# Two of five threshold subtractions per attention pair moved from VectorE to GpSimd, with a new order of all tasks

## The chip, the cores and the metric

The kernel runs on one core of a Trainium2 chip. The metric is the device time of one execution in microseconds; lower is better. The kernel before takes 1224.37 us (median of 3 runs, 1223.91 to 1226.27). TensorE is called PE, its weight loads PEld, VectorE DVE, ScalarE ACT, GpSimd POOL and SyncE SP, as in the profile.

## The reference

An attention block with a threshold is followed by a feed-forward block; everything is float32.

```python
# q, k, v: (8, 8, 576, 64); tau = 0.02
scores = (q @ k.transpose(0, 1, 3, 2)) / 8
thresh = scores.max(-1, keepdims=True) - tau
scores = np.where(scores >= thresh, scores, -1e9)
attn = exp(scores - scores.max(-1, keepdims=True))
o = (attn / (attn.sum(-1, keepdims=True) + 1e-9)) @ v
x = o.transpose(0, 2, 1, 3).reshape(4608, 512)
h = x @ w_in                                   # 512 x 2048
out = (h / (1 + exp(-1.702 * h))) @ w_out      # 2048 x 512
```

## The kernel before, in words

**Attention.** Heads are taken two at a time: 32 pairs, four to a batch. The scores of a pair are computed transposed, key positions on the partitions, and stand in five tiles: tiles 0 to 3 hold 128 partitions x 1152 elements, tile 4 holds 128 x 576. For each pair the steps are:

- `load_qk`, `load_v` (SP issues the DMAs), then `prep` (DVE, L556) or, for pairs 0 to 3, a turn on PE (L565, L568) and copies (L578, L580);
- `scores_run`: PE (L590) into the PSUM pool psA, three buffers of two banks; `keep`: ACT copies each piece into its tile (L607);
- `in_groups`: DVE reduces each tile over groups of 32 (L613), here with max, later with add for the denominators; `over_tiles` (L622), `cross_max` (ACT, L632), `over_halves` (L639);
- `spread_max`: DVE writes the threshold of every query to the tile `mb` (L651), 128 x 576, one buffer for all pairs but 1 and 3;
- `sub`: each score tile minus `mb`, in place (L687); `mask`: ACT, a steep Prelu (L694); `exps`: ACT, Exp (L698);
- `values`: PE multiplies by v (L709) into psA; `place_x`: DVE multiplies by the reciprocal denominators (L813) and writes x, transposed, into the tiles xT.

From pair 7 on, the values of one pair and the scores of the next are interleaved on PE, tile by tile. Below, this stretch of PE is called a joint: 36 instructions of each kind, two records each in the trace.

**Feed-forward.** 18 blocks of 256 rows of x follow the pairs that fill them. The first two are plain products (L875, L886), whose hidden values pass through ACT (L843) and DVE (L892); the others use seven products instead of eight, in both layers, with sums formed on DVE. The first layer is L954, L1127 or L1278, the second L1431 or L1387; ACT copies (L968, L1168, L1292) and DVE adds (L973, L1173, L1295) take the first layer out of PSUM, and `read` (L1453 on DVE, L1446 on ACT) takes the second layer out. In blocks 7 to 12, POOL issues the DMAs that stream a set of weights (`w_flow`, L1104).

**Weights.** At the start, each 128 x 512 piece of w_in and w_out is rounded by two ACT instructions (`cv_power` L520, `cv_power2` L524) and two on DVE (L538, L545).

**Order.** Nothing is ordered by hand. Each step is a task with an engine, a cost in us, a rank and its dependencies; the kernel runs a planner (`run_in_order`) that plays the tasks through, gives each engine, whenever it falls free, the ready task of the lowest rank whose buffers are free, and issues the instructions in the order in which the tasks start. Engines then work through their queues strictly in that order. The rank is the pair's number plus a bias by the name of the step, from the tables EARLY (pairs 0 to 3), SECOND (4 to 7), LATER (the rest), CV (weights), and L_RANK and W_RANK (loads). PE's feed-forward work has the lowest priority and fills what attention leaves. Fillers (`stay_warm`, L1497) stand where the planner sees PE without work in the beginning.

```python
    def sub(n, t):
        s = sT[n, t].rearrange("p u h s -> p u (h s)")
        engine = nc.gpsimd if t in BY_POOL.get(n, ()) else nc.vector
        engine.tensor_tensor(
            out=s, in0=s, in1=mbs[n].unsqueeze(1).to_broadcast(list(s.shape)),
            op=ALU.add if n in BY_DMA else ALU.subtract,
        )
```

`BY_POOL` is empty before. For pairs 1 and 3 to 6 tiles 3 and 4 are subtracted by DMAs that add in memory (`add_row`, L678).

The buffer `mb` also takes the reciprocal denominators (`sums_in`, L785) of pairs 6 to 15 and 28 to 31: the planner lets a task start only if the units it takes of a buffer are free, and another task gives them back.

Of the kernel before, what the change touches and what calls it, by code (L numbers as in the profile page):

```python
# [32 lines left out]
def kernel(  # L33
# [40 lines left out]
    NKT = NK // 2  # L74
# [34 lines left out]
        for x in range(2)  # L109
# [26 lines left out]
    EARLY = {  # L136
        "add_row": 15.24,
        "cross_max": 16.53,
        "exps": 169.66,
        "in_groups": 24.3,  # L140
        "keep": 18.51,
        "load_qk": 52.9,
        "load_v": 77.19,
        "mask": 220.69,
        "one_row": 73.01,
        "over_halves": -24.07,
        "over_tiles": 93.0,
        "place_x": 110.06,
        "row_in": 2.01,
        "row_out": -23.95,  # L150
        "scores_run": 0.25,
        "spread_max": -9.31,
        "spread_sums": 55.95,
        "sub": 109.63,
        "sums_by_pe": 219.69,
        "turn_in": 106.44,
        "turn_rows": -16.16,
        "turned": 157.69,
        "values": 15.27,
    }  # L160
    SECOND = {
        "add_row": 48.97,
        "cross_max": -30.15,
        "cross_sums": 46.61,
        "exps": 425.25,
        "in_groups": 788.95,
        "keep": 52.62,
        "load_qk": -8.72,
        "load_v": 50.95,
        "mask": 273.1,  # L170
        "over_halves": 13.47,
        "over_tiles": 10.11,
        "place_x": -14.67,
        "prep": 130.42,
        "row_in": -47.42,
        "row_out": 60.46,
        "scores_run": -14.82,
        "spread_max": -16.4,
        "sub": 29.57,
        "sums_in": 53.13,  # L180
        "sums_out": -17.8,
        "turn_rows": -30.52,
        "turn_sums": 63.82,
        "values": -7.11,
    }
    LATER = {
        "add2": -163.47,
        "add3": -23.7,
        "copy2": 51.25,
        "copy3": 34.37,  # L190
        "cross_max": 60.81,
        "cross_sums": 61.03,
        "exps": 93.29,
        "in_groups": 10.85,
        "keep": 85.17,
        "load_qk": -13.0,
        "load_v": -2.27,
        "mask": 11.12,
        "over_halves": -26.94,
        "over_tiles": -36.69,  # L200
        "place_x": -13.68,
        "prep": 24.88,
        "s_level1": -6.85,
        "s_level2": -6.85,
        "scores_run": 22.76,
        "silu2": 83.51,
        "spread_max": -74.31,
        "sub": -0.09,
        "sums_in": -524.28,
        "sums_out": -75.26,  # L210
        "turn_sums": 83.71,
        "values": -57.82,
    }
    CV = {
        "cv_end": 69.28,
        "cv_power": -47.14,
        "cv_power2": -20.47,
        "cv_whole": -4.05,
        "load_w": 14.98,
    }  # L220

    LAG = {"PE": 0.26, "DVE": 0.18, "ACT": 0.22, "POOL": 0.18, "SP": 0.1}
# [136 lines left out]
    JOINT = 6  # L359
    SINGLE = 7  # L360
    TURNED = (0, 1, 2, 3)
    BY_POOL = {}

# [68 lines left out]
    def own(n, *pools):  # L432
        return tuple(x + "_apart" for x in pools) if n in APART else pools
# [1105 lines left out]
    for i in range(len(pieces)):  # L1539
        y = 0 if i < NDC else 2 if i < n_in else 4  # L1540
        n = NDC if i < NDC else n_in - NDC if i < n_in else n_in
# [14 lines left out]
        m = task("ACT", 0.75, rank, cv_power, i, after=[a] + over)  # L1556
        m = task("ACT", 0.56, rank, cv_power2, i, after=[m])
        if i in ROUND_BY_ACT:
            a = task("ACT", 0.65, rank, cv_round, i, after=[a])
# [760 lines left out]
            next_blk += 1  # L2320

    crossed = {"max": [], "sums": []}
    L_RANK = (6.9, -26.88, 69.44, 31.9, 9.2, 38.16, 10.43, 63.15, 25.98, 364.83, 169.13, -0.14, 11.11, -6.6, 5.42, 34.59, 27.46, 64.99, 61.43, -2.14, 71.89, -4.67, 27.56, 35.73)

    def load_rank(n, which):
        return L_RANK[3 * n + which] if 3 * n < len(L_RANK) else 0.0
# [16 lines left out]
    for n in range(NP):  # L2343
# [3 lines left out]
        r = float(n)  # L2347
# [102 lines left out]
        if n in BY_DMA:  # L2450
            a = task("DVE", 0.22, r, turn_rows, n, after=[a])
            a = transfer(rq[2], 0.3 + 0.4 * by_sp, task(rq[0], 0.65 * rq[1], r, row_out, n, after=[a]), lag=1.3 + flow)
            spread[n] = task(rq[0], 1.1 * rq[1], r, row_in, n, after=[a], take=own(n, "mb"))
# [115 lines left out]
```

## Time and profile before

| | us | share of the span |
|---|---|---|
| time, median of 3 runs | 1224.37 (1223.91 to 1226.27) | |
| span of the profiled execution | 1224.7 | |
| PE busy | 1206.5 | 99% |
| PEld busy | 995.8 | 81% |
| DVE busy | 1077.1 | 88% |
| ACT busy | 797.6 | 65% |
| POOL busy | 69.3 | 6% |

The profiled execution has no time of its own beside its span; the span stands 0.3 us above the median of the timed runs. Matmuls are pipelined, so a busy PE need not be at its peak. Rows of groups read: line, engine, operation, output and input with their shapes, count, then busy time in us and mean ns of one, then the idle time of the engine just before them and what ended it. Each PE instruction leaves two MATMUL records (the transposes of L565 one). Rows of the timeline read: start, duration, engine, line, operation, operands, count, and in brackets the idle time before. An order of instructions, engine by engine, can be read from the built programs of both kernels; it holds no times.

### The profile page before, as it was taken

The page shows a single profiled execution, that of the slowest core. Times are in us where ns is not written, and L with a number is a line of the kernel's source. Part 1 is how long each engine was busy: PE and PEld are TensorE (multiplying, and loading weights), DVE is VectorE, ACT ScalarE, POOL GpSimd, SP SyncE. Part 2 cuts the span into 40 slices and gives each one's busy share as a digit, 9 for nine tenths or more (in the row PEclk, how much of TensorE's full clock was granted, in tenths as well). Part 3 has the DMA queues.
Part 4 walks back from the last instruction along what each step waited for, and adds up shares of the span by engine and source line. Part 5 has one row for each costly group of instructions (what it writes and reads, how often), then busy time and mean ns, then how long its engine had stood idle before and what let it go on. Part 6 is the DMA issues. An engine that isn't in the chain of part 4 may idle for free.

```text
span 1224.7 us, 26240 instructions
## 1 busy us (share of the span) xinstructions
PE 1206.5 (99%) x10672; PEld 995.8 (81%) x10672; DVE 1077.1 (88%) x1683; ACT 797.6 (65%) x1197; POOL 69.3 (6%) x114
## 2 busy tenths in 40 slices
PE   8999999999999999999999999999999999999998
PEld 5656777797978888888777777787787797999998
DVE  6989998878898998898699977998799989999797
ACT  6999977675765766684686468756875676340340
POOL 0111231100000000000100010001100000000000
PEclk9999999999999999999999999999999999999999
DMA  8957769492323241224423252225322351444443
GB/s 222 249 108 190 173 142 170 103 210 65 93 50 110 49 120 48 75 72 135 101 67 99 66 133 72 59 77 128 92 49 67 87 139 39 139 129 140 140 137 104
DMA packets 201193, 136.09 MB, mean 111 GB/s; under 512 B 146864, under 2 KB 163376, under 8 KB 200944
## 3 DMA queue, kind: packets, MB, share of 16 engines
q1 hardware_dynamic: 189712, 110.21, 34.0%
q0 software_dynamic: 10672, 23.90, 9.4%
q8 instruction: 84, 1.38, 0.5%
q10 hardware_dynamic: 688, 0.30, 0.1%
q14 instruction: 37, 0.30, 0.1%
HBM read 103.28 MB, written 23.75 MB: 104 GB/s over the span
## 4 chain that ended last, share of the span: by engine, by line
PE 88%; ACT 8%; DMA 2%; DVE 1%; issue 1%; SPq 0%; DVEq 0%; ACTq 0%
PE ops L1431 28%; PE pv L709 10%; PE ps L590 10%; PE hps L954 7%; PE hps L1127 7%; PE ps L954 5%; PE ps L1127 5%; PE hps L1278 4%; PE ops L1387 4%; PE ps L1278 3%; PE ps L1387 3%; ACT arena L698 2%; ACT arena L694 2%; PE hps L886 2%; ACT arena L607 2%; DMA arena<-in_moe_w_in_dram 1%
## 5 line engine op out<-in xcount | busy, mean ns | idle before, releaser
L613 DVE TRANSPOSE_TENSOR_REDUCE part<-arena 128x36 f32<-128x1152 f32 x300 | 363.8, 1239 | 52.6 <-ACT arena L607 40.2
L607 ACT COPY arena<-ps 128x576 f32<-128x576 f32 x288 | 171.2, 642 | 95.6 <-PE ps L590 95.5
L694 ACT ACTIVATE arena<-arena 128x1152 f32<-128x1152 f32 (+1 forms) x160 | 164.6, 1064 | 66.6 <-DVE arena L687 66.2
L1431 PE MATMUL ops<-w_out,arena 128*128 128x256 f32 x896 | 203.0, 381 | 0.1
L1431 PEld LDWEIGHTS ops<-w_out,arena 128*128 128x128 f32 x896 | 168.5, 190 | 28.5 <-issue 5.3
L687 DVE TENSOR_TENSOR arena<-arena 128x1152 f32<-128x1152 f32 (+1 forms) x150 | 180.9, 1241 | 0.7
L698 ACT ACTIVATE arena<-arena,shift 128x1152 f32<-128x1152 f32 (+1 forms) x160 | 179.7, 1156 | 1.4
L590 PE MATMUL ps<-arena 64*64 64x288 f32 x2304 | 172.1, 408 | 8.0 <-ACT arena L607 6.1
L709 PE MATMUL pv<-arena 64*64 64x288 f32 x2176 | 159.2, 405 | 0.0
L590 PEld LDWEIGHTS ps<-arena 64*64 64x64 f32 x2304 | 81.9, 132 | 71.5 <-ACT arena L607 29.7
L1431 PE MATMUL ops<-arena 128*128 128x256 f32 x576 | 129.1, 379 | 0.0
L709 PEld LDWEIGHTS pv<-arena 64*64 64x64 f32 x2176 | 80.3, 133 | 53.0 <-issue 9.0
L1431 PEld LDWEIGHTS ops<-arena 128*128 128x128 f32 x576 | 109.2, 190 | 15.8 <-issue 0.9
L1292 ACT COPY arena<-hps 128x512 f32<-128x512 f32 x44 | 25.7, 584 | 59.5 <-PE hps L1278 59.5
L632 ACT ACTIVATE other<-red,minus_gap 32x18 f32<-32x18 f32 x118 | 36.2, 307 | 35.1 <-DVE red L622 33.6
L1104 POOL DMA_DIRECT2D arena<-wrow x36 | 19.5, 540 | 619.0 <-DVE arena L1197 321.8
L886 PE MATMUL hps<-xT,w_in 128*128 128x256 f32 x232 | 51.2, 381 | 0.9 <-DVE arena L892 0.9
L886 PEld LDWEIGHTS hps<-xT,w_in 128*128 128x128 f32 x232 | 43.6, 190 | 8.6 <-DVE arena L892 1.5
L1453 DVE SCALAR_TENSOR_TENSOR osb<-ops,osb 128x256 f32<-128x256 f32 x98 | 39.2, 411 | 11.5 <-PE ops L1431 10.5
L954 PEld LDWEIGHTS hps<-xT,w_in 128*128 128x128 f32 x384 | 44.2, 192 | 1.5 <-issue 0.9
L954 PE MATMUL hps<-xT,w_in 128*128 128x128 f32 x384 | 45.3, 276 | 0.0
L1127 PE MATMUL hps<-xT,w_in 128*128 128x256 f32 x192 | 43.4, 379 | 0.0
(228 smaller groups left out, 1859.9 us busy)
## 6 DMA issues: line engine op xcount, KB each, us to landing
arena<-in_v_dram SPq DMA_DIRECT2D x128, 144.0 KB
arena<-exu SPq DMA_DIRECT2D x42, 256.0 KB
arena<-ext SPq DMA_DIRECT2D x39, 256.0 KB
arena<-wrow POOLq DMA_DIRECT2D x36, 256.0 KB, 3.3
arena<-in_k_dram SPq DMA_DIRECT2D x112, 72.0 KB
arena<-in_q_dram SPq DMA_DIRECT2D x112, 72.0 KB
out_dram<-osb SPq DMA_DIRECT2D x28, 256.0 KB
arena<-row_s SPq DMA_DIRECT2D x48, 144.0 KB
```

Source lines behind the costliest of these rows:

```text
L590: nc.tensor.matmul(ps[ts(c, KT), h, 0:SH], lhsT=mats[n, 1][ts(h, D), ts(j, KT)], rhs=mats[n, 0][ts(h, D), ts(c, SH)], start=True, stop=True,)
L607: nc.scalar.copy(out=sT[n, t][:, u], in_=pss.pop((n, j))[:, :, 0:SH])
L613: nc.vector.tensor_reduce(out=stats[n, op][:, t * 2 * QB : min(2 * t + 2, NK) * QB], in_=sT[n, t].rearrange("p u h (g d) -> p (u h g) d", ...
L687: engine.tensor_tensor(out=s, in0=s, in1=mbs[n].unsqueeze(1).to_broadcast(list(s.shape)), op=ALU.add if n in BY_DMA else ALU.subtract,)
L694: nc.scalar.activation(out=s, in_=s, func=AF.Prelu, alpha=STEEP)
L698: nc.scalar.activation(out=s, in_=s, func=AF.Exp, scale=SCALE, bias=shift)
L709: nc.tensor.matmul(o[c][ts(h, D), 0:SH], lhsT=left(j, h)[ts(c, KT)], rhs=sT[n, t][ts(c, KT), u, h, :], start=(j == 0), stop=(j == NK - 1),)
L886: nc.tensor.matmul(hidden[j][:, ts(i, BLK)], lhsT=w_in[:, c, ts(j, P)], rhs=xTs[i][:, c, :], start=(c == 0), stop=(c == NDC - 1), skip_gro ...
L954: nc.tensor.matmul(o[:, ts(j, HT)], lhsT=left[:, c, ts(4 * y + j, P)], rhs=right[:, c, :], start=(x in (P1, P2, P5) and j + c == 0), stop= ...
L1127: nc.tensor.matmul(o[:, ts(j, BLK)], lhsT=left[:, c, ts(j, P)], rhs=right[:, c, :], start=(x in (P1, P2, P5) and j + c == 0), stop=(j + c ...
L1278: nc.tensor.matmul(o[:, ts(j, HT)], lhsT=left[:, ts(j, P)], rhs=right, start=(m in (P1, P2, P5) and j == 0), stop=(j == 3), skip_group_che ...
L1431: nc.tensor.matmul(banks[blk][k][:, ts(o, HM)], lhsT=left[:, j, :], rhs=right[:, j, :], start=(j == 0), stop=(j == HF - 1),)
```

## The change

For pairs 8 to 31 the subtraction of tiles 3 and 4 is issued on GpSimd; tiles 0 to 2 stay on DVE. The two chains no longer wait for each other, and `mb` counts as two units: `spread_max` takes both, the last subtraction on either engine gives one back. The denominators of later pairs (`sums_in`) still take one unit of `mb`. The planner books a GpSimd subtraction with 2.6 us for a full tile and 1.4 us for the last one. All biases of the ranks have new values, so the order of all tasks on all engines is another one. Which instructions are issued, and on what data, is otherwise the same.

```diff
-    for x in ("raw0", "raw1", "qkT0", "qkT1", "mb"):
+    for x in ("raw0", "raw1", "qkT0", "qkT1"):
         limits[x + "_apart"] = 1
+    limits["mb"] = limits["mb_apart"] = 2
     EARLY = {
-        "add_row": 15.24,
...
+        "add_row": -378.340771,
...
-    BY_POOL = {}
+    BY_POOL = {n: (3, 4) for n in range(8, 32)}
...
-    SHARED = 0.2 if BY_POOL else 0.0
...
-    W_RANK = (51.17, 144.32, 134.71, 686.68, 50.64, 279.44)
+    W_RANK = (-29.011801, 237.669982, 129.549423, 790.056925, 152.018894, 491.392438)
...
-            m = task("DVE", 0.78, r, spread_max, n, after=[a], take=own(n, "mb"))
+            m = task("DVE", 0.78, r, spread_max, n, after=[a], take=own(n, "mb") * 2)
         spread.setdefault(n, m)
-        ws, subs, last_add = [], [(m, None)], spread[n]
+        ws, last_add = [], spread[n]
         mine = ADDED.get(n, ())
+        behind_sub = {False: [m], True: [m]}
+        apart = BY_POOL.get(n, ())
+        by_vector = max(t for t in range(NKT + 1) if t not in mine and t not in apart)
+        by_two = {t: (t == by_vector) * (1 if apart else 2) + (t in apart[-1:]) for t in range(NKT + 1)}
         for t in range(NKT + 1):
...
+                pool = t in BY_POOL.get(n, ())
                 a = task(
-                    "DVE", 0.67 if tail else 1.27, r, sub, n, t, after=[y for y, _ in subs],
-                    give=own(n, "mb") if t == max(set(range(NKT + 1)) - set(mine)) else (),
+                    "POOL" if pool else "DVE", (1.4 if tail else 2.6) if pool else 0.67 if tail else 1.27, r, sub, n, t,
+                    after=behind_sub[pool], give=own(n, "mb") * by_two[t],
                 )
-                subs.append((a, None))
+                behind_sub[pool] = [a]
```

`SHARED` is used nowhere. The tables SECOND, LATER, CV and L_RANK change in the same way as EARLY and W_RANK. All lines of the changed kernel below the tables stand one further on (L590 is L591 there).

More of the change, by code (lines that the diff above doesn't have):

```diff
@@ L129 @@
               "raw0": 1, "raw1": 1, "qkT0": 1, "qkT1": 1, "v_m0": 1, "v_m1": 1, "w64_0": 1, "w64_1": 1, "row": 1, "row_s": 1, "rc": 1}
-    for x in ("raw0", "raw1", "qkT0", "qkT1", "mb"):
+    for x in ("raw0", "raw1", "qkT0", "qkT1"):
         limits[x + "_apart"] = 1
+    limits["mb"] = limits["mb_apart"] = 2
     limits["s_m_apart"] = NKT
     EARLY = {
-        "add_row": 15.24,
[L138 to L159, printed above, removed]
+        "add_row": -378.340771,
+        "cross_max": -51.670843,
+        "exps": -80.990469,
+        "in_groups": 24.707122,
+        "keep": -1679.732271,
+        "load_qk": -47.984891,
+        "load_v": 33.367154,
+        "mask": 240.776887,
+        "one_row": -544.415211,
+        "over_halves": -422.16303,
+        "over_tiles": -1679.661295,
+        "place_x": -112.949767,
+        "row_in": -35.770691,
+        "row_out": 917.119523,
+        "scores_run": -229.318419,
+        "spread_max": 320.427835,
+        "spread_sums": -32.4166,
+        "sub": 92.995208,
+        "sums_by_pe": 328.173046,
+        "turn_in": -142.452702,
+        "turn_rows": -201.348475,
+        "turned": 189.940288,
+        "values": 425.811909,
@@ L160 @@
     }
     SECOND = {
[L162 to L184, printed above, removed]
+        "add_row": 396.291781,
+        "cross_max": 134.376111,
+        "cross_sums": 254.096747,
+        "exps": 627.348081,
+        "in_groups": 1045.488067,
+        "keep": -1628.325603,
+        "load_qk": -155.794522,
+        "load_v": 99.246196,
+        "mask": 508.237893,
+        "over_halves": -20.868516,
+        "over_tiles": -152.960781,
@@ L185 @@
+        "place_x": 955.1794,
+        "prep": 343.422582,
+        "row_in": 96.454434,
+        "row_out": 125.121366,
+        "scores_run": -126.121027,
+        "spread_max": -35.804964,
+        "sub": 211.446055,
+        "sums_in": 50.193475,
+        "sums_out": -11.007232,
+        "turn_rows": 388.794059,
+        "turn_sums": 445.432231,
+        "values": -55.985049,
     }
     LATER = {
[L187 to L209, printed above, removed]
@@ L210 @@
-        "sums_out": -75.26,
-        "turn_sums": 83.71,
-        "values": -57.82,
+        "add2": -1112.316868,
+        "add3": -1680.126556,
+        "copy2": 64.472372,
+        "copy3": -15.546448,
+        "cross_max": -210.684879,
+        "cross_sums": 950.298394,
+        "exps": 665.775135,
+        "in_groups": 26.792662,
+        "keep": -1855.554282,
+        "load_qk": -101.543529,
+        "load_v": -530.802781,
+        "mask": 92.181036,
+        "over_halves": -26.986143,
+        "over_tiles": -46.863265,
@@ L213 @@
+        "place_x": 35.133329,
+        "prep": 730.714298,
+        "s_level1": -38.984452,
+        "s_level2": -38.984452,
+        "scores_run": 22.464676,
+        "silu2": -1261.340063,
+        "spread_max": 9.276515,
+        "sub": -15.906025,
+        "sums_in": -660.343636,
+        "sums_out": 434.369551,
+        "turn_sums": 447.129924,
+        "values": 217.876057,
     }
     CV = {
[L215 to L218, printed above, removed]
@@ L219 @@
-        "load_w": 14.98,
+        "cv_end": 96.689847,
+        "cv_power": 1.711186,
+        "cv_power2": -11.481877,
+        "cv_whole": 14.392341,
+        "load_w": 5.229801,
     }
@@ L2452 @@
             a = transfer(rq[2], 0.3 + 0.4 * by_sp, task(rq[0], 0.65 * rq[1], r, row_out, n, after=[a]), lag=1.3 + flow)
-            spread[n] = task(rq[0], 1.1 * rq[1], r, row_in, n, after=[a], take=own(n, "mb"))
+            spread[n] = task(rq[0], 1.1 * rq[1], r, row_in, n, after=[a], take=own(n, "mb") * 2)
             m = transfer(rq[2], 1.1, spread[n], 0 if by_sp else 1, give=() if n in ADDED else ("row",), lag=rq[3] + flow)
         else:
-            m = task("DVE", 0.78, r, spread_max, n, after=[a], take=own(n, "mb"))
+            m = task("DVE", 0.78, r, spread_max, n, after=[a], take=own(n, "mb") * 2)
         spread.setdefault(n, m)
-        ws, subs, last_add = [], [(m, None)], spread[n]
+        ws, last_add = [], spread[n]
         mine = ADDED.get(n, ())
+        behind_sub = {False: [m], True: [m]}
+        apart = BY_POOL.get(n, ())
+        by_vector = max(t for t in range(NKT + 1) if t not in mine and t not in apart)
+        by_two = {t: (t == by_vector) * (1 if apart else 2) + (t in apart[-1:]) for t in range(NKT + 1)}
         for t in range(NKT + 1):
```

2 lines of the change are left out of this document (1 added, 1 removed).

## The prediction

> **What bounds the kernel now.** I read first the page's line of busy time, then the busy time by stretches, then the timeline where ACT and DVE are full.
>
> ```profile
> span 1224.7 us, 26240 instructions
> PE 1206.5 (99%) x10672; PEld 995.8 (81%) x10672; DVE 1077.1 (88%) x1683; ACT 797.6 (65%) x1197; POOL 69.3 (6%) x114
> ```
>
> ```profile
> 0.00:40.00 40.00, 33.73 (x522) 25.27 (x524) 28.46 (x44) 29.82 (x49) 3.78 (x19) 0.96 0.92 245
> 40.00:105.00 65.00, 59.96 (x840) 34.30 (x832) 57.12 (x94) 64.18 (x87) 12.98 (x19) 1.00 0.67 158
> 105.00:145.00 40.00, 37.82 (x276) 29.17 (x272) 39.04 (x61) 38.24 (x61) 9.80 (x13) 1.00 0.83 193
> 145.00:200.00 55.00, 53.59 (x384) 42.01 (x388) 50.06 (x78) 44.27 (x62) 13.62 (x17) 1.00 0.77 152
> 200.00:1050.00 850.00, 849.90 (x7135) 693.78 (x7127) 745.00 (x1066) 569.44 (x840) 29.13 (x48) 1.00 0.36 90
> ```
>
> The columns are the stretch, its length, the busy time of PE, PEld, DVE, ACT and POOL, the granted clock, the DMA share and GB/s. From 200 to 1050 us PE is idle for 0.1 us: there the time is PE's own work, which the change leaves as it is. All that an order can win lies ahead of 200 us, where PE idles 6.3, 5.0, 2.2 and 1.4 us. There ACT is the bound (64.18 of 65 us), and after it DVE (39.04 of 40). Pair 8, the first with a subtraction on GpSimd, has its values on PE at 271.20 us (row below), where PE is already full. So moving subtractions off DVE takes work from an engine that ends no wait of PE at that place; what moves the time is the new order of the first 200 us, and whatever GpSimd does to DVE behind them.
>
> **The first 100 us.** In the built orders the PE sequence is nearly the same up to the first matmul of the hidden layer (L886). But ahead of the place that this matmul needs, ACT has 140 instructions instead of 138: one `cv_power` and one `cv_power2` more, and the two stand in the stretch in which ACT has no idle time. DVE has 149 instead of 147, one L613 and one L538 more.
>
> ```profile
> L520 ACT ACTIVATE w_in<-w_out,rebias 128x512 f32<-128x512 int16 x12 | 9.3, 773 | 0.8 <-DMA w_out<-in_moe_w_in_dram 0.8
> L524 ACT ACTIVATE w_in<-w_in,rebias 128x512 int32<-128x512 f32 x16 | 11.5, 728 | 0.3
> L613 DVE TRANSPOSE_TENSOR_REDUCE part<-arena 128x36 f32<-128x1152 f32 x240 | 321.7, 1362 | 50.0 <-ACT arena L607 37.5 <-ACT arena L698 11.6
> ```
>
> ```profile
> 111.27 25.95 PE L886 MATMUL hps<-xT,w_in 128*128 128x256 f32 x119 [0.89 <-DVE arena L892]
> ```
>
> ACT: 0.77 + 0.73 = 1.5 us later, and with it the hidden layer's long run, which starts at 111.27 us. DVE's L613, 1.36 us, and a shorter L538 lie in its 7.9 us of idle time (65 - 57.12). I take +1.5 us; from 0, if a wait elsewhere swallows it, to 2.9, if L613 is in the way too (1.5 + 1.36).
>
> **145 to 200 us.** Before the values of pair 6 (194.98 us) the new PE order has 16 instructions L1431 fewer, 24 instead of 40; the ACT order needs as many instructions up to the end of these values as before (256).
>
> ```profile
> 176.11 0.60 ACT L843 ACTIVATE xT<-hps 128x512 f32<-128x512 f32 x1 [3.95 <-PE hps L886]
> ...
> 184.34 4.90 ACT L694 ACTIVATE arena<-arena 128x1152 f32<-128x1152 f32 x5 [0.79 <-DVE arena L687]
> 189.14 5.35 ACT L698 ACTIVATE arena<-arena,shift 128x1152 f32<-128x1152 f32 x5
> ...
> 223.26 4.20 ACT L698 ACTIVATE arena<-arena,shift 128x1152 f32<-128x1152 f32 x4
> ...
> 257.33 3.06 ACT L698 ACTIVATE arena<-arena,shift 128x1152 f32<-128x1152 f32 x3
> ```
>
> ```profile
> 187.98 3.62 PE L1431 MATMUL ops<-w_out,arena 128*128 128x256 f32 x16
> 191.43 3.62 PE L1431 MATMUL ops<-arena,arena 128*128 128x256 f32 x16
> 194.98 1.20 PE L709 MATMUL pv<-arena 64*64 64x288 f32 x16
> ...
> 230.34 1.15 PE L709 MATMUL pv<-arena 64*64 64x288 f32 x16
> ...
> 271.20 1.20 PE L709 MATMUL pv<-arena 64*64 64x288 f32 x16
> ```
>
> ```profile
> L698 ACT ACTIVATE arena<-arena,shift 128x1152 f32<-128x1152 f32 x128 | 157.1, 1253 | 1.3
> ```
>
> Sixteen records start within 191.43 - 187.98 = 3.45 us, 0.216 us each; 16 instructions are 32 records, so PE arrives 6.9 us earlier. The first of the five Exp instructions ends at 189.14 + 1.25 = 190.4 us, 4.6 us ahead of its use. So 6.9 - 4.6 = 2.3 us are missing, unless ACT's idle 3.95 us for PE's hidden block, 0.79 us for DVE and the like get filled. Bounds 0 and 2.3; I take half, +1.2 us. Ahead of pair 7's values PE has 8.6 us less work and DVE 5.0, ahead of pair 8's 17.9 and 10.0 (sums over both orders by the trace's mean durations), so DVE is 3.6 and 7.9 us tighter. The tiles had 230.34 - (223.26 + 1.25) = 5.8 us to spare at pair 7's second tile and 271.20 - (257.33 + 3.06) = 10.8 at pair 8: both fit, and cost nothing.
>
> **Switching between small and full matmuls.**
>
> ```profile
> 312.00 3.77 PE hps L954 x32
> 315.77 3.57 PE ps L954 x32
> ```
>
> In the chain of waits the first full block after a joint takes 0.20 us more than the next. Entries and exits together number 75 instead of 77: -0.2 us.
>
> **DVE and GpSimd behind 200 us.** The subtractions of one pair on DVE:
>
> ```profile
> L687 DVE TENSOR_TENSOR arena<-arena 128x1152 f32<-128x1152 f32 x123 | 162.2, 1349 | 0.7
> L687 DVE TENSOR_TENSOR arena<-arena 128x576 f32<-128x576 f32 x27 | 20.2, 749 | 0.0
> L1475 POOL TENSOR_SCALAR_AFFINE_SELECT eye<-eye 128x128 f32<-128x128 f32 x1 | 0.3, 287 | 0.1
> L1467 POOL MEMSET rebias<- 128x1 f32 x1 | 0.1, 98 | 0.0
> ```
>
> DVE is rid of 162.2/123 + 20.2/27 = 1.32 + 0.75 = 2.07 us a pair. No GpSimd subtraction has been traced. From below: one input at (287 - 98)/127 = 1.49 ns per element gives 1.8 and 1.0 us for the two tiles; from above: two inputs read one after the other, 3.5 and 1.8 us. I take the middle, 2.65 and 1.4, 4.0 us a pair. The Trainium skill (GPSIMD Engine Reference, section 3.1) measures about 2.6 cycles an element at 1.2 GHz for this operation; an estimate from it is 2.5 and 1.25 us, and the sum would be the same.
>
> Beside it DVE has time: tiles 0 to 2 keep ACT busy longer than GpSimd needs. The order, however, puts DVE's first two subtractions right beside GpSimd's two, in all 24 pairs, and further operations with two SBUF inputs behind them. If the engines run side by side, DVE gains 2.07 us a pair, nobody on PE's path needs it, and the effect is zero. If they exclude each other, DVE is held up to 4.0 us a pair, 1.9 us more than it was rid of. The Trainium skill (SBUF — State Buffer, section "SBUF: two separate sides") says that they do: one pair of ports, locked for a whole instruction, wanted by GpSimd and by DVE operations with two SBUF inputs. No run here shows it yet.
>
> What a hold-up costs shows at pair 18, one of the tightest:
>
> ```profile
> 614.13 2.40 ACT L698 ACTIVATE arena<-arena,shift 128x1152 f32<-128x1152 f32 x2
> ...
> 618.53 0.78 ACT L698 ACTIVATE arena<-arena,shift 128x576 f32<-128x576 f32 x1
> ```
>
> ```profile
> 618.71 1.15 PE L709 MATMUL pv<-arena 64*64 64x288 f32 x16
> ...
> 624.84 0.66 PE L709 MATMUL pv<-arena 64*64 64x288 f32 x8
> ```
>
> The tile used at 618.71 is ready at 614.13 + 1.25 = 615.4: 3.3 us to spare. A net 1.9 us fits, a full 4.0 us leaves 0.7 us of stall. DVE's idle time between 200 and 1050 us is 850 - 745 = 105 us, 4.4 us for each of 24 pairs: it catches up within a pair. But DVE also reads PSUM for PE (L1173, L1453), and one such read behind one held subtraction comes up to 2.65 us late, at 24 places. Bounds: nothing, and 24 x 0.7 = 17 us; I take 0.15 us a pair, 3.5 us, near the lower end because the spare time of a typical pair exceeds the net delay.
>
> GpSimd's own queue: in three pairs of the order a weight issue (L1104) stands between the two subtractions.
>
> ```profile
> POOL arena L1104 <- PE ps L1127: 53.6, 11, 10.4
> ```
>
> Such an issue waits for PE 4.9 us on average; tile 4 has 624.84 - (618.53 + 0.78) = 5.5 us to spare at pair 18. I cost it at nothing; were that cover gone, it would be 3 x 4.9 = 15 us. SP's queue is moved little: `sums_in` into `mb` may now have to wait for GpSimd's last subtraction, with the loads of later pairs queued behind it; those are issued a pair ahead, and I cost this at nothing too.
>
> **Sum.** 1224.7 (span) + 1.5 + 1.2 - 0.2 + 3.5 = 1230.7; the span stands 0.3 us above the median, so 1230.4 us.
>
> **Rivals.** (a) Faster: the new order fills PE's idle time between 105 and 200 us, 2.2 + 1.4 = 3.6 us, because ACT's 3.95 us wait falls away, and GpSimd costs nothing: 1224.4 - 3.6 = 1220.8. For it: the PE order has no fillers at the end of the hidden block any more; against it: ACT's additional 1.5 us in its full stretch. (b) No change: ACT's additions are covered and the engines run side by side, 1224.2. It is also the case in which the change does nothing that PE sees, as the 0.1 us of idle time says. (c) Much slower: DVE and GpSimd exclude each other and every pair pays; it decides from the point where the hold-up exceeds 3.3 us of spare time. With the two early terms, 1224.4 + 2.5 + 17 = 1244.
>
> **How the numbers follow.** The forecast, slightly slower, 0.46; (a) 0.2; (b) 0.14; (c) 0.2. 0.2% is 2.4 us, about what a measurement of this kernel can tell from no change. Slower 0.46 + 0.2 = 0.66, same 0.14, faster 0.2. The range leaves out half of (a) and half of (c): 1221 to 1243. The likeliest case alone spans 1226.8 (no cost behind 200 us) to 1236.
>
> **What would show it.** Right: the first L886 block starts 1 to 2 us later than 111.27 us; ACT keeps over 98% between 40 and 105 us; PE waits for L698 or L607 around 190 us; DVE's L687 rows grow beyond 1349 ns where GpSimd's stand beside them, and PE's idle time between 200 and 1050 us grows from 0.1 us to a few. Wrong: PE's idle time ahead of 200 us sums to less than before's 14.9 us (6.3 + 5.0 + 2.2 + 1.4), or DVE's subtractions keep their 1349 ns while GpSimd works, or PE waits on SP's loads.

## The result and the profile after

The changed kernel takes 1279.99 us (median of 4 runs, 1274.65 to 1286.40), the kernel before beside it on the same chip 1224.14 (1223.38 to 1226.27): ratio 1.0455, 95% interval 1.0421 to 1.0489. The prediction, 1230.4 us with a range of 1221 to 1243, was wrong. The sign was right; the price was missed by 50 us. The profiled execution took 1274.65 us, its span is 1272.9.

The first page of the profile after, line of the busy times and the first line of the chain that ended last; then that line of the chain of the kernel before:

```profile
PE 1216.9 (96%) x10672; PEld 997.8 (78%) x10672; DVE 1105.2 (87%) x1635; ACT 799.3 (63%) x1197; POOL 209.3 (16%) x162
...
PE 54%; DVE 21%; ACT 13%; issue 6%; DMA 4%; SPq 1%; DVEq 0%; ACTq 0%; POOL 0%; POOLq 0%
```

```profile
PE 88%; ACT 8%; DMA 2%; DVE 1%; issue 1%; SPq 0%; DVEq 0%; ACTq 0%
```

VectorE has 48 instructions fewer than before (1635 against 1683) and is busy 28 us longer. A fifth of the chain now runs through it, before 1%. The busy times of the changed kernel by the same stretches as in the prediction (stretch, length, then PE, PEld, DVE, ACT, POOL, clock, DMA share, GB/s):

```profile
0.00:40.00 40.00, 35.38 (x565) 25.55 (x568) 30.52 (x46) 32.00 (x52) 6.05 (x23) 1.00 0.95 254
40.00:105.00 65.00, 58.81 (x828) 34.48 (x824) 58.34 (x99) 64.36 (x90) 13.32 (x18) 1.00 0.68 162
105.00:145.00 40.00, 38.59 (x293) 29.59 (x285) 39.61 (x58) 39.60 (x62) 7.94 (x13) 1.00 0.79 188
145.00:200.00 55.00, 52.73 (x395) 41.42 (x394) 52.47 (x80) 44.67 (x64) 14.23 (x18) 1.00 0.72 141
200.00:1050.00 850.00, 814.21 (x6694) 659.54 (x6694) 725.63 (x946) 544.59 (x797) 161.60 (x92) 1.00 0.34 88
```

Ahead of 200 us PE idles 4.6 + 6.2 + 1.4 + 2.3 = 14.5 us, before 14.9: the same. Behind it PE idles 850 - 814.2 = 35.8 us where it had idled 0.1. Most of the time is lost there, in the pairs with GpSimd.

Idle time isn't all of it. The two spans differ by 48.2 us: 37.8 are idle time of PE (56.0 against 18.2) and 10.4 longer busy time (1216.9 against 1206.5). About half of the latter has a cause in the trace: behind three of PE's waits, of 1.97, 3.84 and 2.58 us, the granted clock is 0.50 for 3.41 us. Here is the second of them, the stretch (columns as above) and PE's timeline:

```profile
654.06:657.47 3.41, 3.41 (x10) 2.69 (x9) 3.38 (x4) 3.38 (x4) 0.00 (x0) 0.50 0.00 0
```

```profile
652.84 5.41 PE L1128 MATMUL hps<-arena,w_in 128*128 128x256 f32 x16 [3.84 <-ACT arena L1169]
```

These 16 records take 5.41 us, the next 16 of their line 3.62. The three stretches cost 3 x 3.41 x 0.5 = 5.1 us. The kernel before shows no such stretch behind 200 us. Not every wait is followed by one: that of 2.55 us at 876.91 isn't.

The groups of the subtraction by form, in the changed kernel, and VectorE's largest group beside them:

```profile
L614 DVE TRANSPOSE_TENSOR_REDUCE part<-arena 128x36 f32<-128x1152 f32 x240 | 323.5, 1363 | 72.1 <-ACT arena L608 42.2 <-ACT arena L699 29.1
...
L688 DVE TENSOR_TENSOR arena<-arena 128x1152 f32<-128x1152 f32 x99 | 203.9, 2089 | 0.8
...
L688 POOL TENSOR_TENSOR arena<-arena 128x1152 f32<-128x1152 f32 x24 | 82.8, 3450 | 515.5 <-DVE arena L652 403.4 <-ACT arena L969 77.7 <-DMA arena<-in_q_dram 30.1
L688 POOL TENSOR_TENSOR arena<-arena 128x576 f32<-128x576 f32 x24 | 57.9, 2411 | 0.1
```

(All lines below sub's stand one further down than before.) 24 fewer of VectorE's large subtractions, yet 203.9 us instead of 162.2: the mean grew from 1349 to 2089 ns. The transposing maximum, with one input, kept its time (1363, before 1362). 99 x (2089 - 1350) ns = 73.2 us, or 3.05 us a pair, are added to VectorE's subtractions, more than the 2.07 us a pair that it was rid of (1350 ns is their mean in a run below, in the same order without the exclusion). GpSimd's own are longer too than they are alone, 2.61 us (in the side-by-side kernel below) and 1.42 us (the shortest in this trace).

What follows from it is seen at one pair, here in the timelines of VectorE, GpSimd and PE of the changed kernel (start, duration, engine, line; the bracket is idle time before it and what ended it):

```profile
307.77 5.07 DVE L688 TENSOR_TENSOR arena<-arena 128x1152 f32<-128x1152 f32 x2
312.76 0.74 DVE L1454 SCALAR_TENSOR_TENSOR osb<-ops,osb 128x256 f32<-128x256 f32 x2
313.43 1.90 DVE L688 TENSOR_TENSOR arena<-arena 128x1152 f32<-128x1152 f32 x1
315.25 1.36 DVE L614 TRANSPOSE_TENSOR_REDUCE part<-arena 128x36 f32<-128x1152 f32 x1
316.55 0.38 DVE L1454 SCALAR_TENSOR_TENSOR osb<-ops,osb 128x256 f32<-128x256 f32 x1
```

```profile
307.96 6.16 POOL L688 TENSOR_TENSOR arena<-arena 128x1152 f32<-128x1152 f32 x2 [28.32 <-DVE arena L652]
```

```profile
313.56 2.05 PE L955 MATMUL hps<-xT,w_in 128*128 128x128 f32 x16 [0.39 <-DVE osb L1454]
316.98 2.05 PE L955 MATMUL hps<-xT,w_in 128*128 128x128 f32 x16 [1.37 <-DVE osb L1454]
```

VectorE's two subtractions last 5.07 us instead of 2.7, the third 1.90. Behind them in VectorE's queue stand the reads L1454 that empty a PSUM buffer, and PE needs that buffer: 0.39 and 1.37 us of idle time. Over the whole stretch, the view of PE's waits of the changed kernel from 200 to 1050 us (total us, times, longest; before, this view is empty):

```profile
PE hps L1128 <- ACT arena L1169: 8.8, 5, 3.8
PE hps L955 <- DVE osb L1454: 6.7, 7, 1.9
PE ops L1432 <- DVE osb L1454: 6.4, 8, 2.0
PE ps L591 <- ACT arena L608: 4.5, 6, 1.5
PE hps L955 <- ACT arena L969: 3.7, 2, 1.9
PE hps L1128 <- DVE osb L1454: 2.5, 1, 2.5
PE ps L955 <- DVE arena L974: 2.5, 1, 2.5
PE ps L1128 <- DVE arena L1174: 0.6, 1, 0.6
```

Every line names a read of PSUM, on VectorE or on ACT; none names an Exp (L699) or a DMA. ACT's reads come late the same way, behind masks that wait for subtractions: ahead of PE's wait of 3.84 us shown above, VectorE's three subtractions last 6.99 us from 639.88, ACT's last four masks start only at 645.69, and the copy L1169 that PE needs comes behind them, at 652.22. ACT's waits for the subtractions, first the changed kernel, on VectorE and on GpSimd, then the kernel before, same stretch:

```profile
ACT arena L695 <- DVE arena L688: 93.3, 44, 7.6
...
ACT arena L695 <- POOL arena L688: 1.3, 2, 0.8
```

```profile
ACT arena L694 <- DVE arena L687: 65.4, 24, 6.0
```

### The profile page after: what moved, and what is told of

It reads as the page before. It is cut to its first block, busy times and chain, and to the rows that moved or that the text cites. A ratio compares the mean times of both kernels' runs of the same rounds, so it can differ in the third digit from the quotient of the medians.

```text
span 1272.9 us, 26355 instructions
## 1 busy us (share of the span) xinstructions
PE 1216.9 (96%) x10672; PEld 997.8 (78%) x10672; DVE 1105.2 (87%) x1635; ACT 799.3 (63%) x1197; POOL 209.3 (16%) x162
## 4 chain that ended last, share of the span: by engine, by line
PE 54%; DVE 21%; ACT 13%; issue 6%; DMA 4%; SPq 1%; DVEq 0%; ACTq 0%; POOL 0%; POOLq 0%
PE ops L1432 13%; PE pv L710 7%; DVE arena L688 7%; PE ps L591 7%; DVE part L614 5%; PE hps L955 5%; PE ps L955 4%; PE hps L1279 4%; PE ops L1388 4%; ACT arena L695 4%; ACT arena L699 3%; PE ps L1388 3%; PE ps L1279 3%; ACT arena L608 3%; PE hps L1128 3%
## 5 line engine op out<-in xcount | busy, mean ns | idle before, releaser
L614 DVE TRANSPOSE_TENSOR_REDUCE part<-arena 128x36 f32<-128x1152 f32 (+1 forms) x300 | 364.9, 1239 | 72.1 <-ACT arena L608 42.2
L608 ACT COPY arena<-ps 128x576 f32<-128x576 f32 x288 | 171.1, 642 | 99.0 <-PE ps L591 97.9
L688 POOL TENSOR_TENSOR arena<-arena 128x1152 f32<-128x1152 f32 (+1 forms) x48 | 139.8, 2931 | 515.6 <-DVE arena L652 403.4
L688 DVE TENSOR_TENSOR arena<-arena 128x1152 f32<-128x1152 f32 (+1 forms) x102 | 206.0, 2050 | 0.8
L591 PE MATMUL ps<-arena 64*64 64x288 f32 x2304 | 172.4, 408 | 11.6 <-ACT arena L608 10.0
L699 ACT ACTIVATE arena<-arena,shift 128x1152 f32<-128x1152 f32 (+1 forms) x160 | 178.0, 1153 | 1.1
L591 PEld LDWEIGHTS ps<-arena 64*64 64x64 f32 x2304 | 82.9, 132 | 73.7 <-ACT arena L608 33.3
L1454 DVE SCALAR_TENSOR_TENSOR osb<-ops,osb 128x256 f32<-128x256 f32 x98 | 38.8, 407 | 9.7 <-PE ops L1432 5.7
```

What stands on the lines that cost most here:

```text
L591: nc.tensor.matmul(ps[ts(c, KT), h, 0:SH], lhsT=mats[n, 1][ts(h, D), ts(j, KT)], rhs=mats[n, 0][ts(h, D), ts(c, SH)], start=True, stop=True,)
L608: nc.scalar.copy(out=sT[n, t][:, u], in_=pss.pop((n, j))[:, :, 0:SH])
L614: nc.vector.tensor_reduce(out=stats[n, op][:, t * 2 * QB : min(2 * t + 2, NK) * QB], in_=sT[n, t].rearrange("p u h (g d) -> p (u h g) d", ...
L688: engine.tensor_tensor(out=s, in0=s, in1=mbs[n].unsqueeze(1).to_broadcast(list(s.shape)), op=ALU.add if n in BY_DMA else ALU.subtract,)
L699: nc.scalar.activation(out=s, in_=s, func=AF.Exp, scale=SCALE, bias=shift)
```

## The experiments

Theory L: GpSimd's subtraction and VectorE instructions with two SBUF inputs shut each other out; VectorE's queue stands still, PSUM is emptied late. Rivals: O, the new order is what costs; H, GpSimd is slow and its two tiles come late; S, a shared bandwidth. Each run stands against the kernel before on the same chip (1224.8 to 1225.2 us).

**The disputed cost by itself.** A kernel of its own: 8 instructions of one engine in a row, then the same with the other engine's beside them.

```python
    def dve_sub():    nc.vector.tensor_tensor(out=a, in0=a, in1=a_mb, op=ALU.subtract)      # L46
    def dve_groups(): nc.vector.tensor_reduce(out=part, in_=a..., apply_transpose=True)     # L49
    def dve_read():   nc.vector.scalar_tensor_tensor(out=a_out, in0=ps, ..., in1=a_out)     # L54
    def pool_sub():   nc.gpsimd.tensor_tensor(out=b, in0=b, in1=b_mb, op=ALU.subtract)      # L59
    def pool_one():   nc.gpsimd.tensor_scalar(out=b, in0=b, scalar1=0.0, scalar2=None, op0=ALU.add)   # L62
    def pool_set():   nc.gpsimd.memset(b, 0.0)                                              # L65
```

> A kernel of its own, which leaves the whole computation out and writes zeros: eight instructions each of three forms of VectorE (the subtraction with two inputs in SBUF 128x1152, the transposing maximum over 128x1152 in SBUF, the read of 128x256 and more from PSUM with an addend in SBUF, here 128x512) and of three of GpSimd (subtraction, one input plus a constant, a memset, all 128x1152), first each alone, then in pairs side by side. Theory L (VectorE instructions with two SBUF inputs and GpSimd instructions that read SBUF shut each other out for a whole instruction): alone about 1.34 us for VectorE's and 2.62 us for GpSimd's subtraction; side by side VectorE's takes at least 2.4 us in the mean and the pair together about the sum, 4.0 us, for each turn; VectorE's transposing maximum (1.36 us) and its PSUM read keep their times to 5% beside GpSimd's subtraction; beside a memset VectorE's subtraction keeps 1.34 us. Rival S (they share a bandwidth): every form of VectorE that reads SBUF gets longer beside GpSimd's subtraction, the transposing maximum too, and a memset lengthens the subtraction as well. Rival H (no exclusion, GpSimd is merely slow): all keep their times side by side.

Its timeline, VectorE's subtractions alone, beside GpSimd's subtraction, beside the one-input operation, beside the memset; then GpSimd's three alone and its subtraction beside VectorE's:

```profile
7.95 11.11 DVE L46 TENSOR_TENSOR dve_data<-dve_data,dve_mb 128x1152 f32<-128x1152 f32 x8 [1.13 <-ACT dve_data L41]
...
92.86 27.13 DVE L46 TENSOR_TENSOR dve_data<-dve_data,dve_mb 128x1152 f32<-128x1152 f32 x8 [58.15 <-ACT dve_data L41]
123.35 31.52 DVE L46 TENSOR_TENSOR dve_data<-dve_data,dve_mb 128x1152 f32<-128x1152 f32 x8 [3.35 <-ACT dve_data L41]
155.44 13.40 DVE L46 TENSOR_TENSOR dve_data<-dve_data,dve_mb 128x1152 f32<-128x1152 f32 x8 [0.57 <-ACT dve_data L41]
```

```profile
34.98 21.41 POOL L59 TENSOR_TENSOR pool_data<-pool_data,pool_mb 128x1152 f32<-128x1152 f32 x8 [34.54 <-ACT pool_data L43]
57.20 25.57 POOL L62 TENSOR_SCALAR pool_data<-pool_data 128x1152 f32<-128x1152 f32 x8 [0.80 <-ACT mark L38]
83.52 8.86 POOL L65 MEMSET pool_data<- 128x1152 f32 x8 [0.75 <-ACT mark L38]
93.17 29.30 POOL L59 TENSOR_TENSOR pool_data<-pool_data,pool_mb 128x1152 f32<-128x1152 f32 x8 [0.78 <-ACT pool_data L43]
```

VectorE: 11.11 / 8 = 1.39 us a turn alone; 27.13 / 8 = 3.39 us beside the subtraction (the first one got through at 1.36 us, the other seven took 3.65 each); 31.52 / 8 = 3.94 beside the one-input operation. Beside the memset seven kept 1.36 us; the eighth fell into the next part, beside a subtraction, and took 3.65. Both engines together need 3.68 us a turn, 93% of what the two take one after the other (1.36 + 2.61 = 3.97). The groups of the other two forms, half of each beside GpSimd's subtraction:

```profile
L49 DVE TRANSPOSE_TENSOR_REDUCE part<-dve_data 128x36 f32<-128x1152 f32 x16 | 21.8, 1361 | 1.4 <-ACT mark L40 1.4
...
L54 DVE SCALAR_TENSOR_TENSOR dve_out<-ps,dve_out 128x512 f32<-128x512 f32 x16 | 10.5, 656 | 15.6 <-ACT dve_out L42 15.6
```

They keep their time. This is what theory L expected, but for the 7% by which the turns overlap; S and the part of H that all keep their times are out. The Trainium skill (SBUF — State Buffer, section "SBUF: two separate sides") gives just this rule: one port pair, held for a whole instruction, and for VectorE instructions with two SBUF inputs only against a GpSimd instruction that reads SBUF. The trace agrees, the memset included; "fully blocks" holds up to the 7% by which turns overlap.

**The exclusion taken away, the order kept.** First with one memset in place of each GpSimd subtraction, then with three, so that GpSimd is busy longer than with subtractions that nothing holds up. Both kernels leave the subtraction of these tiles out.

```diff
     def sub(n, t):
+        if t in BY_POOL.get(n, ()):
+            nc.gpsimd.memset(s, 0.0)        # second run: three times
+            return
```

> The changed kernel in which GpSimd, in place of its subtraction, sets the two tiles to zero: the subtraction of tiles 3 and 4 of pairs 8 to 31 is left out, GpSimd writes as much and reads nothing. Theory L, in the form that only a GpSimd instruction that reads SBUF shuts out VectorE's with two SBUF inputs: VectorE's 128x1152 subtractions take 1.34 to 1.45 us throughout, PE's idle time between 200 and 1050 us falls from 35.8 us to under 5, 1216 to 1226 us. Rival O: 1265 us or more, the order being the same. Rival S (any GpSimd access to SBUF slows VectorE): VectorE's subtractions stay over 1.6 us where a memset stands beside them, 1230 to 1260 us.

> The changed kernel in which GpSimd, in place of each of its two subtractions, sets the tile to zero three times over (the subtraction of tiles 3 and 4 of pairs 8 to 31 is left out): at 1.06 us a memset of 128x1152 GpSimd is then busy 3.2 and about 1.6 us, longer than with the subtractions (2.61 and 1.42), but reads nothing from SBUF. Theory L (the exclusion costs the time): as with one memset, 1226 to 1234 us, VectorE's 128x1152 subtractions at 1.35 us. Rival H (tiles 3 and 4 come late because GpSimd is slow): 1265 to 1285 us.

Measured: 1229.42 us (ratio 1.0042, 1.0027 to 1.0056) and 1228.90 (1.0033, 1.0023 to 1.0044). The groups and the stretch from 200 us of the kernel with three:

```profile
L691 DVE TENSOR_TENSOR arena<-arena 128x1152 f32<-128x1152 f32 x99 | 130.6, 1350 | 0.8
...
L689 POOL MEMSET arena<- 128x1152 f32 x72 | 76.4, 1060 | 472.2 <-DVE part L614 469.4
L689 POOL MEMSET arena<- 128x576 f32 x72 | 41.5, 577 | 2.8
```

```profile
200.00:1050.00 850.00, 847.39 (x7064) 693.25 (x7063) 694.47 (x1011) 564.19 (x834) 144.50 (x190) 1.00 0.36 91
```

VectorE's subtractions are at 1350 ns, PE's idle time at 2.6 us, all of it for two of ACT's reads (1.8 us for L608, 0.8 us for L1172). So 1280.0 - 1228.9 = 51 us go with the subtraction on GpSimd. The remaining 4 us against before are the new order's: these 2.6 us and some 1.5 us elsewhere. The second run came out as theory L expected; the first missed its upper bound of 1226 by 3 us, because of the order's 4 us.

On H these two runs say less than was intended. GpSimd takes 3 x (1.06 + 0.58) = 4.9 us a pair, longer than the 4.03 of undisturbed subtractions, but a memset needs no threshold: it waits for the tile's maximum only (L614 in the row above; the subtractions wait for `mb`, L652), and in 19 of the 24 pairs the last memset ends before ACT's first mask of the pair. So lateness of tiles 3 and 4 was hardly tried. What excludes H is the changed kernel itself: ACT waits 1.3 us in all for GpSimd's subtractions (row above), and PE waits for no Exp between 200 and 1050 us.

**The order alone and the engine alone.** In the new order all five tiles on VectorE again (first run); in the old order only the engine of tiles 3 and 4 changed (second).

```diff
-        engine = nc.gpsimd if t in BY_POOL.get(n, ()) else nc.vector     # after
+        engine = nc.vector
```

```diff
-        engine = nc.gpsimd if t in BY_POOL.get(n, ()) else nc.vector     # before
+        engine = nc.gpsimd if n >= 8 and t in (3, 4) else nc.vector
```

> The changed kernel with its new order and its second threshold buffer, in which only the engine of the subtraction is VectorE again for all five tiles. Theory L (the exclusion of VectorE and GpSimd costs the time): VectorE has 2.07 us more work a pair, its subtractions take 1.34 us again, and the hold-ups go: 1218 to 1228 us, at or below the kernel before, since the new order was 5.5 us ahead at 180 us. Rival O (the new order behind 200 us is what costs): 1265 us or more, since the order is the same. Rival H (GpSimd is slow, tiles 3 and 4 come late): 1218 to 1228 as well, so the other runs have to tell L and H apart.

> The kernel before with its old order and its single threshold buffer, in which only the engine of the subtractions of tiles 3 and 4 of pairs 8 to 31 is GpSimd. Theory L: VectorE's 128x1152 subtractions beside GpSimd's take at least 2.3 us in the mean, VectorE's reads of PSUM come late, 1240 to 1275 us. Rival O (it is the new order): 1224 us within 3. Rival H (GpSimd is slow, tiles 3 and 4 come late to ACT and PE): VectorE's subtractions keep 1.35 us, PE waits for ACT's Exp at the joints, 1224 to 1240 us.

The second: 1277.06 us (1.0438, 1.0412 to 1.0464), just above the expected 1240 to 1275 and as slow as the changed kernel. The engine alone does it; the new order has taken nothing off. Its groups, and then two of them in the kernel before:

```profile
L687 DVE TENSOR_TENSOR arena<-arena 128x1152 f32<-128x1152 f32 x99 | 181.6, 1857 | 0.7
...
L687 POOL TENSOR_TENSOR arena<-arena 128x1152 f32<-128x1152 f32 x24 | 82.1, 3423 | 506.8 <-DVE arena L651 444.7 <-DMA arena<-in_q_dram 62.1
...
L1054 DVE TENSOR_TENSOR arena<-arena 128x512 f32<-128x512 f32 x22 | 20.1, 952 | 0.0
...
L934 DVE TENSOR_TENSOR arena<-xT,arena 128x256 f32<-128x256 f32 x12 | 11.3, 942 | 0.1
```

```profile
L1054 DVE TENSOR_TENSOR arena<-arena 128x512 f32<-128x512 f32 x22 | 14.0, 678 | 0.0
...
L934 DVE TENSOR_TENSOR arena<-xT,arena 128x256 f32<-128x256 f32 x12 | 5.0, 418 | 0.1
```

VectorE's subtractions of pairs 8 to 31 (72 of the 99) take 1349 + 99 x (1857 - 1349) / 72 = 2048 ns in the mean, less than the 2.3 us that was expected. In this order a part of the hold-up falls on VectorE's additions with two SBUF inputs instead: these two groups and those of L1197 are 25 us longer than before. With the subtractions that makes (50.3 + 25.1) / 24 = 3.14 us a pair, as much as in the changed kernel.

The first: 1248.64 us (1.0197, 1.0173 to 1.0221), which neither theory had expected (1218 to 1228, or 1265 and more). This order was planned for a VectorE with three subtractions a pair; with five it stands 2.07 us a pair longer ahead of its reads, and that costs 1248.6 - 1228.9 = 19.7 us, 0.8 us a pair, without any subtraction on GpSimd. That is of the size of the prices below.

**The price of a delay on VectorE.** To the kernel with three memsets, additional maxima over 128x512 on VectorE, whose results nobody uses: five a pair, then two. Then two a pair in the kernel before. And GpSimd subtracting tile 4 only, tile 3 set to zero three times.

```diff
+        for i in range((2, 2, 1)[t] if n >= 8 and t < 3 else 0):     # then: 1 if n >= 8 and t < 2
+            x = work.tile([P, 16], FP32, name="idle", tag="idle", bufs=1)
+            nc.vector.tensor_reduce(out=x, in_=sT[n, t]...[:, 0:512]..., op=ALU.max, apply_transpose=True)
```

> The same as the kernel with three memsets, and on VectorE two, two and one additional transposing maxima over 128x512 behind the subtractions of tiles 0, 1 and 2 of pairs 8 to 31, whose results nobody uses: some 0.65 us each, 3.2 us a pair, about as much as the exclusion held VectorE up (3.07 us a pair), with no exclusion at all. Theory L (what costs is only that VectorE's queue stands still about 3 us a pair ahead of its reads of PSUM): 1260 to 1285 us. Rival C (VectorE catches up in its idle time, and the time was lost by something else beside GpSimd): 1228 to 1240 us.

> The kernel with three memsets for each GpSimd subtraction (those of tiles 3 and 4 of pairs 8 to 31 are left out), and on VectorE one additional maximum over 128x512 behind the subtractions of tiles 0 and 1 of these pairs, 1.3 us a pair instead of the 3.2 us that cost 65 us. In proportion: 1229 + 0.4 x 65 = 1255 us, from 1245 to 1262. If VectorE swallows it: at most 1236 us.

> The kernel before, nothing on GpSimd, with the same additional 1.3 us a pair on VectorE (one maximum over 128x512 behind the subtractions of tiles 0 and 1 of pairs 8 to 31). If VectorE's queue has no room for a delay whatever the order (theory L's reason for the price): 1240 us or more. If the old order has the 3.3 us to spare that the prediction read at the joints: 1224 to 1230 us.

> The changed kernel's order; on GpSimd tile 3 is set to zero three times (its subtraction is left out for pairs 8 to 31) and only tile 4 is subtracted, so GpSimd holds VectorE up for 1.42 us a pair instead of 4.03. Theory L, in proportion: 1229 + 0.35 x 51 = 1247 us, from 1238 to 1255. Rival T (a hold-up of about one microsecond a pair is swallowed): at most 1234 us.

The groups that give the delays: the five maxima (the pairs of maxima have the same mean, 712 and 711 ns), and VectorE's subtractions with tile 4 alone on GpSimd:

```profile
L697 DVE TRANSPOSE_TENSOR_REDUCE idle<-arena 128x16 f32<-128x512 f32 x120 | 85.4, 712 | 4.1
```

```profile
L692 DVE TENSOR_TENSOR arena<-arena 128x1152 f32<-128x1152 f32 x99 | 147.5, 1520 | 0.8
```

Delay of VectorE a pair, and cost a pair (the excess over 1228.9 us, in the old order over 1224.8, divided by 24; the times of one kernel's runs lie 2 to 12 us apart, which is 0.1 to 0.5 us a pair from the lowest to the highest):

| run | time, us | delay a pair | cost a pair |
|---|---|---|---|
| tile 4 on GpSimd: 99 x (1520 - 1350) ns / 24 | 1234.39 | 0.70 us | 0.23 us |
| two maxima: 2 x 0.712 | 1242.75 | 1.42 | 0.58 |
| the changed kernel | 1279.99 | 3.05 | 2.13 |
| five maxima: 5 x 0.712 | 1293.98 | 3.56 | 2.71 |
| two maxima in the kernel before | 1237.02 | 1.42 | 0.51 |
| old order, tiles 3 and 4 on GpSimd | 1277.06 | 3.14 | 2.18 |

The changed kernel lies on the line that delays without any GpSimd subtraction draw, and PE's waits in the kernel with five maxima name the same reads: the first microsecond costs a third to two fifths, what goes beyond 1.4 us nearly all, (2.13 - 0.58) / (3.05 - 1.42) = 0.95. A part of this steepness is the granted clock, in the mean 0.998 with two maxima, 0.996 in the changed kernel and 0.989 with five. So it is the length of the hold-up that counts, not who causes it, and the old order has no more room than the new one.

In none of these four runs did theory L's range hold, although its mechanism did. Five maxima cost more than theory L's 1260 to 1285 us; the delay was longer than planned, 3.56 instead of 3.2 us. Linear scaling failed for the small delays (1247 and 1255 us were expected, 1234.4 and 1242.8 came). Tile 4 alone came out where rival T had put it (at most 1234 us), with a hold-up of only 0.70 us; at 1.42 us the swallowing fails, 1242.8 against at most 1236. In the kernel before 1237.0 lies between the two forecasts, 1224 to 1230 and 1240 or more: the delay isn't swallowed, but costs less than expected.

**Other plans.** Only the last tile on GpSimd with an order planned for it; and no subtraction on GpSimd, with the new early tables and the old later ones.

```diff
-    BY_POOL = {n: (3, 4) for n in range(8, 32)}
+    BY_POOL = {n: (4,) for n in range(8, 32)}       # second run: {}, and SECOND, LATER of before
```

> The changed kernel with only the last, half-sized tile of pairs 8 to 31 on GpSimd, and the order planned for that. Theory L: GpSimd holds the lock 1.42 us instead of 4.03 us a pair, 0.35 of it; by that share of the 50 us that the exclusion costs (1280.0 less 1229.4 us) 1238 to 1250 us. Rival T (hold-ups up to about 1 us a pair are swallowed, only longer ones cost): 1224 to 1232 us.

> No subtraction on GpSimd; the new tables for the first layer, conversions and weight loads and the second threshold buffer are kept, the two tables of the later layers are those of before, and the order is planned anew with them. If the new early order is worth the 2.7 us by which the changed kernel was ahead at the end of its first 200 us: 1219 to 1223 us. If that lead was the scatter of single executions: 1223 to 1228 us. Neither theory on GpSimd has a stake in it.

1252.11 us (1.0220, 1.0201 to 1.0239) and 1242.31 (1.0143, 1.0126 to 1.0161). Both missed: the first lies 2 us above theory L's 1238 to 1250, the second far above 1219 to 1228. Without any GpSimd subtraction a mixture of tables is 17 us slower than before, so such a plan's time says little of one cause. In the first, VectorE's four subtractions a pair take 1535 ns in the mean, a hold-up of 123 x (1535 - 1349) / 24 = 0.95 us a pair; by the table that is some 0.35 us a pair or 8 us, an estimate, and the rest of its 27 us is probably its order, which no run shows by itself. No run was faster than the kernel before; PE idles there for 15 us ahead of 200 and 0.1 us behind, and neither of these two plans lowers the former (15.4 and 16.3 us).

## Why the prediction was wrong, step by step

**The bound.** Right: PE is full from 200 us on, so freeing VectorE could win nothing there. With the exclusion gone VectorE has 51 us less to do there than before (694 against 745) and the kernel still isn't faster.

**The first 100 us, +1.5 us.** Right, as far as the traces show it, but not to be read from one trace. The first long block of the hidden layer, foretold 1 to 2 us later than 111.27, in the changed kernel, in the kernel with three memsets (the same order up to there) and in the old order with GpSimd:

```profile
109.70 24.44 PE L887 MATMUL hps<-xT,w_in 128*128 128x256 f32 x112 [1.41 <-DVE arena L893]
```

```profile
111.88 24.44 PE L890 MATMUL hps<-xT,w_in 128*128 128x256 f32 x112 [1.24 <-DVE arena L896]
```

```profile
107.94 26.17 PE L886 MATMUL hps<-xT,w_in 128*128 128x256 f32 x120 [0.89 <-DVE arena L892]
```

One and the same order starts this block 2 us apart, and so does the old one (111.27, 107.94). The granted clock sorts the traces. The kernel before has a stretch of 3.41 us at 0.50 at 31.7 us, the kernel with three memsets one at 104.7; the changed kernel and the old order with GpSimd have none ahead of the block. Without such a stretch the old order starts the block at 107.94 and 108.50 us (the latter with two maxima), the new one at 109.70, 109.96, 110.01 and 110.42: later by 1.8 us in the mean. With one, the old order starts it at 111.27, the new one at 111.61, 111.88 and 112.27. So the sign given for being right, later than 111.27, fails in the changed kernel's trace (109.70), but that compares a trace of the kernel before with such a stretch and one of the changed kernel without. ACT was as full as foretold (64.36 of 65 us).

**The values of pair 6, +1.2 us.** Ahead of them PE does wait, 2.27 us in the changed kernel and 2.57 with three memsets, by the upper bound of that term (2.3):

```profile
181.48 3.72 PE L1432 MATMUL ops<-arena 128*128 128x256 f32 x16 [2.27 <-ACT osb L1447]
```

But the wait is for a read of PSUM on ACT (L1447), not for an Exp; the prediction had looked only at the Exp, so that the number came near was luck. In return a wait of the old order is gone, here in PE's timeline of the kernel before:

```profile
146.21 1.25 PE L590 MATMUL ps<-arena 64*64 64x288 f32 x16 [1.52 <-ACT arena L607]
```

By PE's idle time ahead of 200 us in this one pair of traces (14.5, before 14.9) the prediction's own sign of failure came true. Over all traces it didn't: the old order idles 14.9, 12.9 and 12.9 us there, the new one 14.5 to 17.4 in seven traces. The sum of the early terms, 2.7 us, fits this, and it is small: all that the new order costs by itself is 4 us.

**GpSimd's subtraction, 2.65 and 1.4 us.** Right in the number: 2.61 and 1.42 alone. The working behind it was luck: its lower bound took 1.8 us for one input, and an operation with one input took 3.13 us, longer than the subtraction with two.

**The exclusion.** Weighed as possible, with the consequence right: VectorE held for up to 4.0 us a pair. 3.05 us a pair were measured. The case "no cost behind 200 us", 1226.8 (1226.9 by its own terms), is the kernel with memsets: 1228.9.

**The hold-ups' price, 0.15 us a pair, 3.5 us in all: this step failed.** It was 2.13 us a pair, 51 us, and even the upper bound of 17 us and rival (c)'s 1244 were far too low. Three things in it were wrong. The spare time was read at the joint, 3.3 us between an Exp and its use, but between 200 and 1050 us PE waits nowhere for an Exp; it waits for reads of PSUM that stand behind the held subtractions. The prediction named these reads and their delay, "up to 2.65 us late, at 24 places", which is 64 us, and then left that out of its bounds. Second, it set the hold-up against the 2.07 us that VectorE was rid of: with two maxima a pair VectorE has 0.65 us less to do than in the kernel before, and still pays 0.58 us. Third, "it catches up within a pair", from 4.4 us of mean idle time a pair: the idle time lies where VectorE waits for others (44.5 of the 105 us ahead of maxima that wait for ACT), and a delay of 1.42 us in the kernel before costs 0.51 us of PE's time.

**The queues of GpSimd and SP, nothing.** Right: no wait of PE behind 200 us names them. VectorE waits 10.3 us for the DMA of the denominators there, in the kernel before not at all; but it does so as long with three memsets (10.1), so this belongs to the order.

**The rivals.** (c), with a chance of 0.2, had the mechanism; the point from which it decides was set at 3.3 us, and the table shows a cost from 0.7 us on. (a) and (b) are out: no part of the change gains anything PE can use.

## What to carry to other kernels

The room of an in-order queue is the smallest slack of anything that stands in it, here the reads that empty PSUM, not the engine's mean idle time and not the slack of the moved step. When work moves to an engine that may shut out another, price the hold-up at every place by what is queued behind it, and let that product be the upper bound. A small kernel that runs the two instructions side by side shows the exclusion; the kernel with writes in place of the moved work separates it from the order; and added work of known length on the held engine gives the price. Whether the moved work comes late itself is read from who waits for it. Compare early times of two traces only where the granted clock agrees.

## What the runs showed of the hardware

The side-by-side kernel showed that GpSimd's one-input addition of a constant takes longer than its two-input subtraction (3.13 against 2.61 us for 128x1152), and that VectorE's subtraction takes longer beside it (3.92 against 3.65 us). A memset of the same size takes 1.06 us and holds up nothing. The hold-up works both ways: GpSimd's subtraction grew from 2.61 to 3.60 us beside VectorE's. In the changed kernel three of PE's waits of 2 to 4 us were followed by 3.41 us at a granted clock of 0.50, so a hold-up there cost twice.
